# The forward convolution of a two-layer SSM kernel, reordered: tables between h chunks, table turns between spectra, the first norm of q inside the convolution, two residuals inside the inverse

## The chip, the cores and the metric

The kernel runs on one core of one Trainium2 chip. The metric is the device time of one launch in microseconds (us), the median of three runs: 986.35 us before the change (981.84, 986.35 and 989.6). One launch computes the forward pass of four layers and the gradients of all ten inputs. Engines are named as in the profile: PE (TensorE), DVE (VectorE), ACT (ScalarE), POOL (GpSimd), SP (SyncE, which here only issues DMAs).

## The reference, cut to what matters

```python
def A(q, k, v, shift_k, ssm_k, ssm_D):             # S = 2048 tokens, D = 512 channels
    k_shift = short causal conv of k with shift_k, four taps
    kv = k_shift * v
    y = irfft(rfft(kv padded to 2S) * rfft(ssm_k padded to 2S))[:S] + kv * ssm_D
    return q * y

def B(x, w1, b1, w2, b2):                          # F = 1376
    return gelu(x @ w1 + b1) @ w2 + b2

x = A_q
x = x + A(layernorm(x), A_k, A_v, ...)             # layer 0
x = x + B(layernorm(x), ...)                       # layer 1
x = x + A(layernorm(x), A_k, A_v, ...)             # layer 2, the same k, v and filter
x = x + B(layernorm(x), ...)                       # layer 3
# returned: x, and its vjp with grad_out for q, k, v, shift_k, ssm_k, ssm_D, w1, b1, w2, b2
```

The convolution's result y doesn't depend on x, so it is computed once for layers 0 and 2. Layer 0 then is: norm of q, times y, plus q.

## The kernel before, in words

The kernel has four phases: the forward convolution (`phase_conv_forward`), the forward pass of the layers and then the backward pass (both in `phase_mlp`), and the backward convolution with the weight gradients in its gaps. The change is to the first phase and to the start of the second.

**The transform.** The Fourier transform of length 4096 is done with matmuls. The tokens lie in four blocks of 512; the second half of each block is held in reversed order, which is why q, v and grad_out are first copied in DRAM with some rows reversed (`flip_rows`, one DMA of 1 MB each). The frequencies are cut into five groups by their rest k1 (`GROUPS`, 2, 2, 4, 4 and 4 tiles of 128 frequencies). For each group DVE combines blocks to "streams" (class `Fold`: tiles fold_x, fold_s, fold_d, fold_t), and PE multiplies them with a table of cosines and sines (`fwd_group`: PSUM tile sp_ps, evicted by ACT). There are two tables: tabN at integer positions, for the filter ssm_k (called h), and tabF at half positions, for kv. `sin_of` makes a quarter of a table: POOL and DVE compute phases into tab_u, DVE masks them, ACT takes the sine. For the way back the tables are needed transposed: `turn_table` makes tabI from tabF, `turn_integer_table` makes tabG from tabN, with transposes on PE and evictions on ACT or DVE.

**The order of phase one.** Tables tabN and wdiag (the short filter as diagonals); `h_chunk` for each of four channel chunks, which turns h (hA, hR), and the reversal of hR (hB); small tables sp5; the fold of h; `k_slice` for four blocks of k, which turns k; then

```python
    h_group(0)
    h_group(1)
    for i in range(4):
        ks_slice(i)
    h_group(2)
    ...                                      # tabF, turn_integer_table
    h_group(3)
    h_group(4)
```

`h_group` makes a group of spectra of h in pairs of tiles (Hg, two buffers) and stores each pair to DRAM (Hspec) from SP's queue. `ks_slice` does the short convolution with 64 small matmuls per block, multiplies with v on DVE to kv and stores ks from POOL's queue; v and ks have two buffers each (vt, ksb). kv is kept in the memory of y (tile y_res). Then tabI is turned, and the loop over the groups runs: load the h spectra (Hg of the inverse), `fwd_group` for kv (KVg), `inv_group` of the group before (iv_ps to W), `product` of the two spectra (pr_t, pr_u to Yg, one buffer), and the streams of a later group. At the end class `InvBlocks` sums up W on DVE and writes y, block by block.

**The start of phase two.** `phase_mlp` turns the weights on PE, then runs four lanes, one for each block of 512 tokens, interleaved by hand-set weights. A lane loads its part of q (x_sl), does the norm (`ln_slice`: bn_stats and bn_aggr on DVE, a power of -0.5 on POOL, scale and shift on DVE or ACT), stores the normalised n for the backward pass, multiplies with y and adds x (`a_fwd`), norms again, turns n by DMA, and does the dense layer with its gelu in groups of four 128-row chunks (`b_fwd`, `gelu_group`).

**What sets the order.** A scheduler places instructions, but PE and DVE work in phase one goes through the `Ordered` wrapper, which keeps the order of the program. Its helper is line 55, so all these instructions carry L55 in the profile and are told apart by their tiles. In phase one the name `tt` is taken from the plain engine, so the kv product (L491) is placed by the scheduler. Pools opened with `reuse_waits="tile"` wait only for the tiles whose memory they take over; others wait for the whole pool that had the memory.

Of the kernel before, what the change touches and what calls it, by code (L numbers as in the profile page):

```python
# [71 lines left out]
def ssm_kernel(ctx, tc: tile.TileContext, aps: dict):  # L72
# [10 lines left out]
    res.rstd = [const_pool.tile([P, NT], F32, name=f"rstd{i}") for i in range(4)]  # L83
    dram = Dram()
# [4 lines left out]
    dram.tabI = drampool.tile([P, 2, 16, 256], BF16, name="tabI_d")  # L89
# [11 lines left out]
    flip_rows(nc, dram.qB, qf, 511)  # L101
# [71 lines left out]
def sin_of(nc, consts, pool, out, krow, pv, shift, np_=P):  # L173
    n = krow.shape[-1]
    for c0 in range(0, n, 1024):
        w = min(1024, n - c0)
        u = pool.tile([P, 1024], I32, name="tab_u", tag="tab_u", bufs=2)[0:np_, 0:w]
        eng = nc.gpsimd if c0 == 0 else nc.vector
        eng.tensor_scalar(out=u, in0=krow[:, c0:c0 + w], scalar1=pv, scalar2=float(shift), op0=ALU.mult, op1=ALU.add)
        nc.vector.tensor_single_scalar(out=u, in_=u, scalar=8191, op=ALU.bitwise_and)  # L180
        nc.scalar.activation(out=out[:, c0:c0 + w], in_=u, func=ACT.Sin, scale=SIN_SCALE, bias=consts.pibias[0:np_, :])


def turn_table(nc, psum, consts, tab, dest, f, qt):

    for k0 in (0, 8):
        ps = psum.tile([P, 8, P], BF16, name="tt_ps", tag="kt", bufs=2)
        for k in range(8):
            nc.tensor.transpose(out=ps[:, k, :], in_=tab[:, f, qt, (k0 + k) * P:(k0 + k + 1) * P], identity=consts.ident)
        if f == 0:  # L190
            nc.scalar.activation(out=dest(k0), in_=ps, func=ACT.Identity)
        else:
            nc.vector.tensor_copy(out=dest(k0), in_=ps)


def turn_integer_table(nc, psum, pool, consts, tabN, dest):

    for f in range(2):
        for k0 in (0, 8):
            tg = pool.tile([P, 8, 2, P], BF16, name="tg", tag="kn", bufs=4)  # L200
            for qt in range(2):
                ps = psum.tile([P, 8, P], BF16, name="tn_ps", tag="kt", bufs=2)
                for k in range(8):
                    nc.tensor.transpose(out=ps[:, k, :], in_=tabN[:, f, qt, (k0 + k) * P:(k0 + k + 1) * P],
                                        identity=consts.ident)
                nc.scalar.activation(out=tg[:, :, qt, :], in_=ps, func=ACT.Identity)
            nc.gpsimd.dma_start(out=dest[:, f, k0:k0 + 8, :].rearrange("p k (t q) -> p k t q", t=2), in_=tg)
# [24 lines left out]
class Fold:  # L232


    def __init__(self, nc, pool, lo, hi, integer, X=None):
        tt = nc.vector.tensor_tensor
        self.nc, self.pool, self.integer = nc, pool, integer
        if X is None:
            X = pool.tile([P, 2, 4, 1024], BF16, name="fold_x", tag="fold_x", bufs=1)
# [61 lines left out]
def product(nc, pool, A, B, Rb, g, out, conj):  # L301
# [4 lines left out]
    for h in range(0, n, 2):  # L306
        s = slice(h, h + 2)
        t = pool.tile([P, 2, 2, 512], BF16, name="pr_t", tag="pr_t", bufs=2)
# [8 lines left out]
        tt(out=out[:, 0, s], in0=t[:, 0], in1=t[:, 1], op=op_r)  # L317
        tt(out=out[:, 1, s], in0=u[:, 0], in1=u[:, 1], op=op_z)
# [16 lines left out]
def inv_group(nc, psum, tabI, Y, g, W):  # L335
    k1, base, n = GROUPS[g]
    sr, sz = SLOT[k1]
    for m in range(2):
        q = slice(m * P, (m + 1) * P)
        for slot, (a, b) in ((sr, (0, 1)), (sz, (1, 0))):  # L340
# [3 lines left out]
            for kt in range(n):  # L344
                nc.tensor.matmul(ps[:, 0, :], lhsT=tabI[:, 0, base + kt, q], rhs=Y[:, a, kt, :], start=(kt == 0),
                                 stop=(kt == n - 1))
            for kt in range(n):
                nc.tensor.matmul(ps[:, 1, :], lhsT=tabI[:, 1, base + kt, q], rhs=Y[:, b, kt, :], start=(kt == 0),
# [46 lines left out]
def phase_conv_forward(ctx, nc, tc, dims, consts, dram, res, aps):  # L395
# [3 lines left out]
    h_ap = aps["A_ssm_k"]  # L399
    tt = nc.vector.tensor_tensor  # L400
    nc = Ordered(nc, tc, ("tensor", "vector"))
# [5 lines left out]
    wpool = res.wstack.enter_context(tc.tile_pool(name="wfwd", bufs=1, side="right"))  # L407
    rstack = ExitStack()
    tabs = rstack.enter_context(tc.tile_pool(name="cf_tab", bufs=1, side="right"))
    tabF = tabs.tile([P, 2, 2, 2048], BF16, name="tabF")  # L410
    foldp = rstack.enter_context(tc.tile_pool(name="cf_fold", bufs=1, side="right"))
    gen = ExitStack()
# [10 lines left out]
    hN = foldp.tile([P, ND * S + 16], BF16, name="hN", tag="fold_x", bufs=1)  # L423
    nc.vector.memset(hN[:, ND * S:ND * S + 16], 0.0)
    for cc in range(ND):
        nc.sync.dma_start(out=hN[:, cc * S:(cc + 1) * S], in_=h_ap[cc * P:(cc + 1) * P, :])
    for i in range(4):
# [5 lines left out]
    flip_rows(nc, dram.vB, v_ap, 511)  # L433

    krow = gp.tile([P, 2048], F32, name="krow")
    for k1, base, n in GROUPS:
        ki = gp.tile([P, 1024], I32, name="krow_i", tag="tab_u", bufs=2)[:, 0:n * P]
        nc.gpsimd.iota(ki, pattern=[[8, n * P]], base=k1, channel_multiplier=0)
        nc.vector.tensor_copy(out=krow[:, base * P:(base + n) * P], in_=ki)
# [10 lines left out]
    for qt in range(2):  # L450
        for f in range(2):
            sin_of(nc, consts, gp, tabN[:, f, qt, :], krow, pvn[:, qt:qt + 1], 2048 * (1 - f))
    wshf = gp.tile([P, ND, 4], F32, name="wshf")
    nc.vector.tensor_copy(out=wshf, in_=wsh)
    wdiag = gp.tile([P, ND, 4, P], BF16, name="wdiag")
    for cc in range(ND):
        for j in range(4):
            nc.vector.tensor_scalar(out=wdiag[:, cc, j, :], in0=consts.ident, scalar1=wshf[:, cc, j:j + 1],
# [878 lines left out]
```

## Time and profile before

| | of 985.4 us |
|---|---|
| PE busy | 803.6 (82%) |
| DVE busy | 729.5 (74%) |
| ACT busy | 611.6 (62%) |
| POOL busy | 152.5 (15%) |
| mean DMA rate | 180 GB/s |
| first spectrum of h on PE | starts at 51.6 |
| first spectrum of kv on PE | starts at 154.6 |
| last write of y on DVE | ends at 232.8 |
| first gelu operation on DVE | starts at 268.8 |
| last forward matmul of the chain | ends near 495 |

The table's lower half is read from the instructions in order of time. A share of busy time over the whole span says little here, since the phases have different limits: until 100 us the tables and the turns of k and h, then the transforms, then the layers. What an edit is worth has to be read from the stretch it lies in: which engine is full there, and which wait ends last. Idle time in front of an instruction stands in square brackets in the timeline, with what ended it.

### The profile page before, as it was taken

How to read it: one execution, taken by the hardware profiler on the slowest of the kernel's cores; microseconds unless marked ns; L12 is line 12 of the kernel's file. 1: busy time of each engine (PE TensorE's matmuls, PEld its weight loads, DVE VectorE, ACT ScalarE, POOL GpSimd, SP SyncE). 2: the span in 40 equal slices, each digit the busy share in tenths (PEclk: the TensorE clock that was granted, in tenths of full speed). 3: DMA queues.
4: the chain of work that ended last, by engine and by line, in shares of the span. 5: the costliest groups of instructions: out<-in, count | busy, mean ns of one | idle time of the engine just before them, and what ended most of it. 6: DMA issues, size and time to landing. Idle time of an engine off the chain costs nothing.

```text
span 985.4 us, 12825 instructions
## 1 busy us (share of the span) xinstructions
PE 803.6 (82%) x4677; PEld 411.7 (42%) x4754; DVE 729.5 (74%) x1207; ACT 611.6 (62%) x806; POOL 152.5 (15%) x271
## 2 busy tenths in 40 slices
PE   0686867984378777777899999978999998995998
PEld 0443424442133322333344444434455554853664
DVE  6624508787899999995847778895369997499873
ACT  5734724642599888987964654535566557753664
POOL 5421100000221112210001112222010304210000
PEclk9867988987698887898999999979999999997999
DMA  6067636303435555468699886647346688863331
GB/s 213 23 214 240 235 122 249 144 27 108 128 109 163 155 161 160 127 191 234 186 302 261 239 222 199 202 145 282 134 160 229 221 318 293 290 200 81 113 97 37
DMA packets 153415, 177.72 MB, mean 180 GB/s; under 512 B 50117, under 2 KB 133768, under 8 KB 152712
## 3 DMA queue, kind: packets, MB, share of 16 engines
q1 hardware_dynamic: 141816, 136.75, 45.0%
q0 software_dynamic: 11536, 40.15, 11.2%
q8 instruction: 37, 0.61, 0.3%
q14 instruction: 26, 0.21, 0.1%
HBM read 92.61 MB, written 82.13 MB: 177 GB/s over the span
## 4 chain that ended last, share of the span: by engine, by line
PE 38%; DVE 35%; ACT 9%; DMA 7%; issue 5%; POOL 4%; SPq 1%; ACTq 0%; DVEq 0%; POOLq 0%
PE sp_ps L55 8%; PE gh_ps L1013 6%; PE gn_ps L1031 6%; DVE Wb L55 6%; PE dw_ps L55 5%; DVE ln_st L897 3%; PE gh_ps L55 3%; DVE b1a L55 2%; DVE g_o L967 2%; PE iv_ps L55 2%; DMA Hspec_d<-Hg 2%; DMA kTc<-kT_d 2%; DMA tabFb<-tabF_d 2%; DVE pr_u L55 2%; PE dw_tp L55 1%
## 5 line engine op out<-in xcount | busy, mean ns | idle before, releaser
L55 PE MATMUL dw_ps<-G,dw_tm 128*128 128x512 bf16 x672 | 167.9, 385 | 4.8 <-ACT dw_tm L1133 3.0
L1133 ACT ACTIVATE dw_tm<-dw_tp 128x1024 bf16<-128x1024 bf16 x88 | 89.9, 1024 | 70.7 <-PE dw_tp L55 70.7
L996 PE MATMUL o_ps<-w_sb,h_sl 128*128 128x512 bf16 x343 | 95.3, 421 | 39.7 <-DVE h_sl L966 38.8
L984 PE MATMUL z_ps<-nT_sl,w_sb 128*128 128x512 bf16 x346 | 83.4, 395 | 20.7 <-DMA nT_sl<-n_sl 19.1
L55 PEld LDWEIGHTS <-dw_tm 128*128 128x128 bf16 x704 | 65.3, 99 | 64.1 <-ACT dw_tm L1133 3.7
L1015 ACT ACTIVATE gz_sl<-gh_ps 128x512 bf16<-128x512 f32 x88 | 50.2, 594 | 55.4 <-PE gh_ps L1013 52.2
L1031 PE MATMUL gn_ps<-w1T_sb,gz_sl 128*128 128x512 bf16 x345 | 80.7, 379 | 0.6 <-DVE gz_sl L1016 0.3
L1013 PE MATMUL gh_ps<-gT_sl,w2T_sb 128*128 128x512 bf16 x344 | 79.1, 379 | 0.5
L996 PEld LDWEIGHTS <-h_sl 128*128 128x128 bf16 x352 | 36.5, 107 | 93.7 <-DVE h_sl L966 44.7
L984 PEld LDWEIGHTS <-w_sb 128*128 128x128 bf16 x352 | 35.0, 101 | 73.5 <-DMA nT_sl<-n_sl 28.3
L986 ACT ACTIVATE g_z<-z_ps,b1col 128x512 bf16<-128x512 f32 x88 | 54.2, 688 | 12.7 <-PE z_ps L984 12.7
L55 PEld LDWEIGHTS <-dw_fm 128*128 128x128 bf16 x704 | 48.3, 100 | 21.5 <-issue 1.9
L55 PE MATMUL dw_tp<-ident,dw_fm 128*128 128x128 bf16 x704 | 55.3, 223 | 0.0
L962 ACT ACTIVATE g_s<-g_t 128x2048 bf16<-128x2048 bf16 (+1 forms) x24 | 42.5, 1771 | 18.2 <-DVE g_t L961 18.2
L1031 PEld LDWEIGHTS <-gz_sl 128*128 128x128 bf16 x352 | 34.3, 98 | 42.0 <-DVE gz_sl L1016 1.0
L1013 PEld LDWEIGHTS <-w2T_sb 128*128 128x128 bf16 x352 | 34.3, 98 | 41.2
L55 DVE TENSOR_REDUCE b1a<-dw_fm 128x1 f32<-128x2048 bf16 x22 | 49.6, 2279 | 0.0
L900 POOL TENSOR_SCALAR rstd<-ln_mv 128x4 f32<-128x4 f32 x16 | 11.4, 715 | 233.1 <-DVE ln_mv L898 148.8
L1043 POOL TENSOR_SCALAR bb_diag<-ident,bb_cols 128x128 bf16<-128x128 bf16 x32 | 21.6, 674 | 152.7 <-DVE bb_junk L1040 143.6
L897 DVE BATCH_NORM_STATS2 ln_st<-x_sl 128x6 f32<-128x512 bf16 x64 | 42.0, 670 | 2.9 <-DMA x_sl<-in_A_q_dram 2.8
L1016 DVE TENSOR_TENSOR gz_sl<-gz_sl,gpb 128x2048 bf16<-128x2048 bf16 (+1 forms) x24 | 27.2, 1135 | 21.5 <-DMA gpb<-gp_d 11.4
L959 ACT ACTIVATE g_q<-g_z 128x2048 bf16<-128x2048 bf16 (+1 forms) x24 | 42.8, 1783 | 0.1
(289 smaller groups left out, 1633.2 us busy)
## 6 DMA issues: line engine op xcount, KB each, us to landing
dw_fm<-h_d SPq DMA_DIRECT2D x22, 512.0 KB, 5.1
dw_fm<-gz_d SPq DMA_DIRECT2D x22, 512.0 KB, 3.8
n_d<-n_sl SPq DMA_DIRECT2D x16, 512.0 KB, 3.6
h_d<-h_sl SPq DMA_DIRECT2D x16, 512.0 KB, 2.9
gp_d<-g_p SPq DMA_DIRECT2D x16, 512.0 KB, 3.2
nb_sl<-n_d SPq DMA_DIRECT2D x16, 512.0 KB, 4.6
gpb<-gp_d SPq DMA_DIRECT2D x16, 512.0 KB, 5.8
gz_d<-gz_sl SPq DMA_DIRECT2D x16, 512.0 KB, 4.9
```

The source lines that it names most:

```text
L55: return self.tc.keep_in_program_order(f(*args, **kwargs))
L897: nc.vector.bn_stats(out=st, in_=x[:, t, :])
L959: nc.scalar.activation(out=q, in_=zb, func=ACT.Square)
L962: nc.scalar.activation(out=sg, in_=t, func=ACT.Sigmoid)
L984: nc.tensor.matmul(ps, lhsT=w.w1[:, dc, c * P:(c + 1) * P], rhs=nT[:, dc, :], start=(dc == 0), stop=(dc == ND - 1))
L986: nc.scalar.activation(out=zb[:, c - c0, :], in_=ps, func=ACT.Identity, bias=w.b1col[:, c:c + 1])
L996: nc.tensor.matmul(ps, lhsT=h[:, c, t * P:(t + 1) * P], rhs=w.w2[:, c, :], start=False, stop=(c == NFC - 1))
L1013: nc.tensor.matmul(ps, lhsT=w.w2T[:, dc, c * P:(c + 1) * P], rhs=gT[:, dc, :], start=(dc == 0), stop=(dc == ND - 1))
L1015: nc.scalar.activation(out=gz[:, c, :], in_=ps, func=ACT.Identity)
L1016: nc.vector.tensor_tensor(out=gz[:, c0:c0 + k, :], in0=gz[:, c0:c0 + k, :], in1=gp[:, 0:k, :], op=ALU.mult)
L1031: nc.tensor.matmul(ps, lhsT=gz[:, c, t * P:(t + 1) * P], rhs=w.w1T[:, c, :], start=(c == 0), stop=(c == NFC - 1))
L1133: nc.scalar.activation(out=dst, in_=ps, func=ACT.Identity)
```

## The change

It moves work within the forward convolution, and pulls the start of layer 0 into it. Part by part:

- One quarter of tabN is made ahead of each `h_chunk`, wdiag behind them. tab_u gets three buffers, and DVE's masks are done in reversed order.
- The streams of h are made ahead of the groups that use them. h groups 0 and 1 stand behind ks slices 0 and 1; a quarter of tabF is made behind each ks slice.
- All table turns become a list of units (`table_turns`), four behind each pair of h tiles in groups 2 and 3. tabI is four tiles in the memory of vt and ksb.
- Stores of h spectra are issued from ACT instead of SP. The products of kv go through the ordered engine.
- q is loaded into the memory of kv once it is folded, normed there (`norm_load`, `norm_sums`, `norm_apply`) and stored as n; lanes 2 and 3 behind the first kv spectrum, lanes 0 and 1 inside the loop.
- Yg is split into halves with three buffers; pr_t has one buffer instead of two. The weights are loaded from inside the loop's program (`start_weights`), and the two small DVE operations on them come later (`finish`).
- `first_sum` does the product with y, the residual and the statistics of the second norm for lanes 0 and 1 between the sums of the inverse. x of all lanes is one tile, loaded in the loop into the memory of fold_x.
- Three pools of phase two wait by tile instead of by pool, and the backward pass has a pool of its own for g_sl.

It is meant to keep PE and DVE supplied in the front part and to take the first norm out of the start of the layers. The diff, cut to its core:

```diff
@@ sin_of
-        u = pool.tile([P, 1024], I32, name="tab_u", tag="tab_u", bufs=2)[0:np_, 0:w]
+        u = pool.tile([P, 1024], I32, name="tab_u", tag="tab_u", bufs=3)[0:np_, 0:w]
...
@@ phase_conv_forward
-    tt = nc.vector.tensor_tensor
     nc = Ordered(nc, tc, ("tensor", "vector"))
+    tt = nc.vector.tensor_tensor
...
-    for qt in range(2):
-        for f in range(2):
-            sin_of(nc, consts, gp, tabN[:, f, qt, :], krow, pvn[:, qt:qt + 1], 2048 * (1 - f))
...
     for cc in range(ND):
+        qt, f = cc // 2, cc % 2
+        sin_of(nc, consts, gp, tabN[:, f, qt, :], krow, pvn[:, qt:qt + 1], 2048 * (1 - f))
         h_chunk(cc)
...
+    sth = [fh.streams(GROUPS[0][0]), fh.streams(GROUPS[1][0])]
...
+    turns = table_turns(nc, psum, gp, consts, tabN, dram.tabG, tabF, tabI, dram.tabI)
+
+    def h_group(g, nturns=0):
         k1, base, n = GROUPS[g]
-        st = fh.streams(k1)
         for h0 in range(0, n, 2):
             H = hrot.tile([P, 2, 2, 512], BF16, name="Hg", tag="Hg", bufs=2)
-            fwd_group(nc, psum, tabN, st, g, H, extra, h0, h0 + 2)
-            nc.sync.dma_start(out=dram.Hspec[:, :, base + h0:base + h0 + 2, :], in_=H)
+            fwd_group(nc, psum, tabN, sth[g], g, H, extra, h0, h0 + 2)
+            nc.scalar.dma_start(out=dram.Hspec[:, :, base + h0:base + h0 + 2, :], in_=H)
+            for _ in range(nturns):
+                turns.pop(0)()
...
-    h_group(0)
-    h_group(1)
     for i in range(4):
         ks_slice(i)
-    h_group(2)
...
+        if i < 2:
+            h_group(i)
+        if i in (1, 3):
+            sth.append(fh.streams(GROUPS[(i + 3) // 2][0]))
+        tabF_part(i)
...
+    h_group(2, 4)
+    h_group(3, 4)
+    sth.append(fh.streams(GROUPS[4][0]))
...
     h_group(4)
-    res.w = start_weights(nc, wpool, dims, aps)
...
+    norm_load(2)
+    norm_load(3)
     load_spec(0)
     load_spec(1)
...
-    sts = [fk.streams(GROUPS[0][0]), fk.streams(GROUPS[1][0])]
+    sts = [fk.streams(GROUPS[0][0])]
+    spectrum(0)
+    norm_sums(2)
+    norm_sums(3)
+    norm_apply(2)
+    norm_load(0)
+    norm_apply(3)
+    norm_load(1)
+    sts.append(fk.streams(GROUPS[1][0]))
...
-        Ys.append(invp.tile([P, 2, 4, 512], BF16, name="Yg", tag="Yg", bufs=1))
-        product(nc, invp, KV, H, Rb, g, Ys[g], False)
+        Ys.append([invp.tile([P, 2, 2, 512], BF16, name="Yg", tag="Yg", bufs=3) for _ in range(n // 2)])
+        product(nc, invp, KVs[g], H, Rb, g, Ys[g], False)
...
+        if g == 0:
+            norm_sums(0)
+            norm_sums(1)
+            res.w = start_weights(nc, wpool, dims, aps)
+        if g == 1:
+            norm_apply(0)
+            norm_apply(1)
+        if g == 2:
+            res.w.finish()
+    res.x = res.xpool.tile([P, NT, D], BF16, name="x_sl", tag="fold_x", bufs=1)
+    for s in range(4):
+        tok_io(nc, res.x[:, s * TS:(s + 1) * TS, :], aps["A_q"].flatten_outer_dims(), dram.qB, s)
...
+    def first_sum(s):
+        x, n = res.x[:, s * TS:(s + 1) * TS, :], ns[s % 2]
+        tt(out=n, in0=n, in1=res.y[:, s * TS:(s + 1) * TS, :], op=ALU.mult)
+        tt(out=x, in0=n, in1=x, op=ALU.add)
+        res.ln1[s] = norm_stats(nc, invp, res.mhalf, x, res.rstd[1], s, res.nmr1[:, s * TS:(s + 1) * TS])
+
+    res.ln1 = {}
+    first_sum(0)
     for m in range(2):
         ib[m].others()
-        for i in range(1, 4):
+    for i in range(1, 4):
+        for m in range(2):
             ib[m].out(i, yv[:, :, m], yv[:, :, 2 + m])
+        if i == 1:
+            first_sum(1)
@@ phase_mlp
-        m.small = st.enter_context(tc.tile_pool(name="m_small", bufs=2))
-        m.spool = st.enter_context(tc.tile_pool(name="m_s", bufs=1))
-        m.hpool = st.enter_context(tc.tile_pool(name="m_h", bufs=1))
+        m.small = st.enter_context(tc.tile_pool(name="m_small", bufs=2, reuse_waits="tile"))
+        m.spool = st.enter_context(tc.tile_pool(name="m_s", bufs=1, reuse_waits="tile"))
+        m.hpool = st.enter_context(tc.tile_pool(name="m_h", bufs=1, reuse_waits="tile"))
...
-                x = m.spool.tile([P, TS, D], BF16, name="x_sl", tag=f"x{s}", bufs=1)
-                tok_io(nc, x, q_ap, dram.qB, s)
+                x = res.x[:, s * TS:(s + 1) * TS, :]
```

## The prediction, written before the result was known

> **What bounds the kernel now.** I first cut the span into stages by what they compute and asked for the busy time of every engine in each (columns: stretch, length, then busy us and instruction count of PE, PEld, DVE, ACT and POOL, granted clock, DMA share, GB/s).
>
> ```profile
> 0.00:51.60 51.60, 18.24 (x141) 13.06 (x142) 33.26 (x83) 32.45 (x52) 26.71 (x69) 0.89 0.33 113
> 51.60:103.90 52.30, 43.73 (x320) 23.29 (x322) 15.93 (x19) 23.51 (x30) 8.19 (x17) 0.72 0.65 228
> 103.90:154.60 50.70, 35.70 (x208) 17.87 (x210) 19.15 (x28) 22.17 (x23) 3.23 (x6) 0.83 0.47 176
> 154.60:213.00 58.40, 50.66 (x213) 21.70 (x218) 46.65 (x68) 30.69 (x36) 0.00 (x0) 0.94 0.43 162
> 213.00:232.90 19.90, 14.65 (x110) 8.68 (x111) 19.42 (x36) 11.17 (x18) 0.00 (x0) 0.83 0.00 1
> 232.90:268.80 35.90, 14.11 (x64) 5.91 (x63) 26.44 (x61) 13.05 (x19) 8.53 (x20) 0.71 0.51 150
> 268.80:330.00 61.20, 44.52 (x172) 18.37 (x177) 58.71 (x89) 58.28 (x60) 12.55 (x16) 0.86 0.45 140
> ```
>
> The rows are: tables and the turning of h; spectra of h and the short conv; the rest of the h spectra with the table turns; spectra of kv, products and inverse (called the loop below); the inverse's last sums; first norms and residuals up to the first gelu operation; gelu of the first lanes. PE has most to do in rows two to four, DVE is full in row five, DVE and ACT both are in row seven. Nothing is full in row six, a start-up of 35.9 us.
>
> Then I read the chain of waits in order of time: in rows two and three it passes through stores.
>
> ```profile
> 50.31 1.24 DVE fold_t L55
> 70.24 7.51 DMA ks_d<-ksb
> 119.12 13.23 DMA Hspec_d<-Hg
> 142.43 3.04 DMA Hspec_d<-Hg
> 223.61 2.02 DVE y_res L55 x6
> 234.74 4.05 DMA x_sl<-qB_d
> 239.09 1.06 POOL rstd L901
> ```
>
> One 512 KB store of h spectra takes 13.2 us, while the list of issues has 3.8 us as its median. The next h spectra wait for its buffer, and the inverse pool waits for the last store. The same stretch among the waits shows who paid, and the timeline shows that the loop's end is tied by one product buffer:
>
> ```profile
> DVE tabI L55 <- DMA Hg<-Hspec_d: 25.1, 1, 25.1
> ACT Hg L298 <- DMA Hspec_d<-Hg: 8.2, 1, 8.2
> 200.78 0.69 DVE L55 TENSOR_TENSOR Yg<-pr_t 128x1024 bf16<-128x1024 bf16 x1 [6.63 <-PE iv_ps L55]
> 205.07 3.15 PE L55 MATMUL iv_ps<-Yg,tabI 128*128 128x512 bf16 x7 [2.93 <-DVE Yg L55]
> ```
>
> DVE stood still for 25.1 us before the table copies. The product of the last group waited 6.6 us for PE to let go of the one Yg; then PE waited 2.9 us for that product.
>
> [...] the 13.2 us store was issued on SP at 119.1, behind the reversed copy of grad_out issued on SP at 111.9, while the transfer rate lay near 100 GB/s. [...] a 128x512 matmul takes 0.38 us from 98 us on and 0.6 us after the 5.2 us pause at 133; but from 51.6 to 98 us the PE stays slow although it is nearly always busy, so I don't count on a better clock. [...] tensor_tensor in bf16 takes 1224 ns at 2048 elements. The trace has 1.22 us.
>
> **The change part by part.**
>
> 1. Tables between h chunks. In row one DVE makes all integer tables (10.6 to 22.0), then wdiag (to 24.9), then the evictions of hA from 25.1, so that PE stands idle for 18 us. Interleaved, a round costs 2.1 us of tables and 1.7 of evictions on DVE, 2.3 and 1.2 on ACT: four rounds end near 25, wdiag near 28, hB's eight evictions (4.3 us of ACT) near 30. The third tab_u buffer shortens the ten small sp5 rounds (37 to 42 now). fold_x starts near 35 instead of 43.5, and its 9 us lie beside the k slices (13 us of ACT, 30 to 43) and the first ks slice, which now precedes the first h group. PE starts this work near 43 instead of 51.6: 8.5 us.
>
> 2. Rows two and three. The matmuls and turns are the same, 79.4 us of PE busy time in 103 us; 23.6 are idle. By the waits: 3.8 for a ks buffer, 4.1 for fold_d, 3.0 for the turns behind ACT, 4.7 for turns behind tabI (held by the last Hspec store), 1.9 for fold_t, 5.2 for an Hg buffer. The new order (ks slices between h groups, turns behind each h pair, stores from ACT, tabI in the vt and ksb slots) puts other matmuls into each of these. New waits: v's third load stands on SP behind the lane of the first two Hspec stores, which lands it near 78; behind it on DVE stand the third kv product and the table work that ACT needs between two Hg evictions, so ACT and then PE lose 3 to 5 us. Each of eight stores costs ACT an issue, of the order of the 0.5 us that SP shows; ACT has 46 us of work here in 103. I take 4 us. The loop starts 8.5 + 23.6 - 4 = 28 us earlier, near 126.6.
>
> 3. The norm of q. Per lane: four stats at 0.66 us (in step with their aggregates), four applies at 0.35: 4.1 us. Lanes 2 and 3 (8.2 us) run while PE does the last two h groups and DVE has nothing: free. Lanes 0 and 1 lie in the loop, with 1.4 us of weight memsets and b2 work: 9.6 us more on a DVE that has 46.7 of 58.4. The second product is queued behind the 6.2 us of stats and memsets, and PE's inverse of group 1 and the spectrum of group 3 wait for it: PE falls some 5 to 8 us behind, and gets back 3.7 of its last waits from Yg in three halves. DVE's sum, 56 us, still fits. I book 3 us of loss (0 to 7). x for the residual is loaded into fold_x after the last streams, hidden by 20 us of loop.
>
> 4. Two residuals in the inverse. Row five is all DVE. It gains 2 x (2.46 for two tensor_tensor + 2.65 of stats) = 10.3 us: 30.2 instead of 19.9.
>
> 5. Row six. No load (2.8 us), no POOL waits for the norm of q (2.3, 2.1 and 2.1), no norm of q, and lanes 0 and 1 done. DVE goes into the residual of lane 2 at once. ACT's order puts the first normalisation of lane 2 in front of the first g_z, so that the first gelu operation waits for: residual of lane 2 and statistics with part of lane 3's, 6.6 us; POOL, 2; three n_sl, five g_z and one g_q on ACT, 8. That is 16.6 instead of 35.9: 19.3 gained.
>
> 6. Row seven. Before, DVE still does all of lane 3's first norm and residual here (6.6) and the second statistics of lanes 2 and 3 (about 4.4): 11 us less in a stretch where DVE had 58.7 of 61.2. But ACT has 58.3: I count the 11 because ACT too comes ahead (n_sl of lanes 0 to 2 are behind it).
>
> Sum: 28 - 3 - 10.3 + 19.3 + 11 = 45 us. Backward and weight gradients don't change in work: their 493 us move up whole. 986.35 - 45 = 941.
>
> **The rivals.** (a) PE stays slow for the whole front and the turns don't fit: row three's warm 10.3 us per four h tiles becomes the 14.4 of group 2 for two groups and the 16 turns take 0.95 instead of 0.65 us, 8 + 5 = 13 us lost: 954. For it: clock 0.72 in row two. Against: row three ran warm until its stop. (b) ACT bounds row seven and part 6 gives nothing, with some loss in the loop (7 rather than 3) and half of (a): 941 + 11 + 4 + 7 = 963. For it: 58.3 of 61.2. (c) PE warms up because it no longer pauses: the four ks slices (5.5 us each) and the first two h groups (12.3 together) at 0.38/0.6 of their time and group 2 at row three's 10.3 save 8 + 4.5 + 4 = 16.5: 925. For it: the slow stretch is preceded by pauses. (d) Slower. [...] at 7.5 us (as for ks_d above) for eight stores that is 60 us, with the 9.6 us of the loop exposed: 941 + 60 + 7 = 1008. [...]
>
> **How the numbers follow.** Forecast 0.50, (a) 0.19, (b) 0.12, (c) 0.14, (d) 0.05. The likeliest gives 941. The range 923 to 965 takes in (a), (b) and (c) and leaves (d) out; with the spread of the forecast itself some 0.16 lies outside. One per cent is 976.5: all but (d) and the edge of (b) lie below. Faster 0.92, same 0.04, slower 0.04.
>
> **What would show it.** Part 1: first h spectrum's fold_x near 35, first ks matmul near 43. Part 2: first KVg near 128, no Hspec store over 6 us, PE idle under 10 us before it. Part 3: q's stats of lanes 2 and 3 in front of the first product with no PE wait behind; a PE wait for Yg of group 1 in the loop. Parts 4 and 5: inverse sums of about 30 us and first g_t 16 to 17 us behind them. Part 6: ACT, not DVE, without gaps after the first g_s. It is wrong if ACT shows waits between Hg evictions for DMA, or if the start of the backward (now at 492) doesn't move up by 35 us or more.

## The result, and the profile after

The changed kernel takes 956.33 us (median of 4 runs, 954.27 to 959.16), the kernel before 984.66 us in the same comparison: a ratio of 0.971 with a 95% interval of 0.966 to 0.976. It is 28 us faster; forecast were 45, with 941 us and a range of 923 to 965. The profiled spans are 985.4 and 952.4 us, 33 us apart; the sums below use these. (The profiled execution after is the shortest of its four runs and the one before lies above the median of its own, hence 33 and not 28.)

The stages of the changed kernel, in the columns of the table shown for the kernel before. Rows one to six are the same work, with the stretches moved to where each stage now begins: start, h spectra and short conv, rest of h and table turns, loop, the inverse's last sums, start of the layers up to the first gelu operation. The last three rows are the forward layers from there on.

```profile
0.00:45.40 45.40, 21.37 (x142) 14.85 (x143) 34.58 (x83) 31.39 (x51) 26.44 (x65) 1.00 0.61 205
45.40:80.00 34.60, 29.61 (x324) 20.56 (x323) 19.71 (x25) 23.51 (x31) 11.67 (x21) 0.98 0.68 237
80.00:117.60 37.60, 33.59 (x208) 14.70 (x207) 22.31 (x39) 24.39 (x26) 8.73 (x17) 0.97 0.85 312
117.60:180.30 62.70, 51.75 (x249) 22.90 (x249) 56.52 (x97) 33.93 (x40) 4.22 (x8) 1.00 0.64 219
180.30:211.50 31.20, 16.97 (x112) 9.30 (x111) 30.38 (x56) 12.69 (x22) 6.33 (x8) 0.79 0.19 51
211.50:227.80 16.30, 11.49 (x38) 4.29 (x38) 10.28 (x22) 10.66 (x16) 4.34 (x8) 0.78 0.38 89
227.80:290.00 62.20, 48.73 (x197) 20.08 (x197) 54.10 (x65) 58.94 (x61) 2.38 (x4) 0.92 0.47 146
290.00:380.00 90.00, 68.10 (x277) 27.89 (x275) 81.23 (x120) 78.41 (x82) 8.63 (x18) 0.87 0.44 138
380.00:462.80 82.80, 59.93 (x242) 24.84 (x243) 58.18 (x73) 63.62 (x70) 5.56 (x11) 0.86 0.61 176
```

Read the PE and clock columns of rows two and three first: 63.2 us of PE work in 72.2, where before it was 79.4 in 103, and a granted clock of 0.98 and 0.97 instead of 0.72 and 0.83. Then the last two rows: in the last one neither PE, DVE nor ACT is full, and in the one before it DVE comes nearest, with 81.2 of 90 us.

The chain of waits in order of time (start, length, what) no longer passes through a store in the convolution; it ends in the layers at a DMA turn:

```profile
45.40 4.83 PE ks_ps L55 x64
...
107.46 10.20 PE sp_ps L55 x40
117.69 1.03 ACT Hg L314
...
217.94 1.17 POOL rstd L989
...
303.48 1.87 SPq L1043
305.40 2.70 DMA nT_sl<-n_sl
308.35 3.59 PE z_ps L1087 x8
```

Stage by stage, in us (the stretch is counted here from the start of the first gelu operation to the end of the last forward matmul):

| | before | after | change | forecast |
|---|---|---|---|---|
| start to the first kv spectrum | 154.6 | 117.6 | -37.0 | -28 |
| loop | 58.4 | 62.7 | +4.3 | +3 |
| last sums of the inverse | 19.9 | 31.2 | +11.3 | +10.3 |
| start of the layers | 35.9 | 16.3 | -19.6 | -19.3 |
| first gelu to last forward matmul | 226.5 | 235.0 | +8.5 | -11 |
| rest (backward) | 490.1 | 489.6 | -0.5 | 0 |
| sum | 985.4 | 952.4 | -33.0 | -45 |

So the first gelu operation comes 41 us earlier, more than the 34 forecast, and 8.5 us are given back in the 235 us behind it. The waits of that stretch (engine and line, what it waited for, us in total, times, longest) say where. First of the kernel before:

```profile
PE z_ps L984 <- DMA nT_sl<-n_sl: 12.1, 6, 4.5
ACT g_z L986 <- PE z_ps L984: 5.3, 6, 3.3
```

Then of the changed one:
```profile
ACT g_z L1089 <- PE z_ps L1087: 27.6, 11, 7.9
PE z_ps L1087 <- DMA nT_sl<-n_sl: 27.2, 5, 8.3
```

PE waits 27 us for turned activations, ACT then waits 28 us for PE. These are waits on the way of one lane from its first dense layer to the second (residual, two norms, DMA turn), when nothing of the other lanes stands ready ahead of it. The experiments ask why; they will show too that the sum of such waits doesn't tell how long the stretch is.

### The profile page after: what moved, and what is told of

Same layout as the page of the kernel before. It is cut to its first block, busy times and chain, and to the rows that moved or that the text cites. A ratio compares the mean times of both kernels' runs of the same rounds, so it can differ in the third digit from the quotient of the medians.

```text
span 952.4 us, 12919 instructions
## 1 busy us (share of the span) xinstructions
PE 794.6 (83%) x4754; PEld 406.6 (43%) x4754; DVE 734.0 (77%) x1203; ACT 613.5 (64%) x810; POOL 151.7 (16%) x274
## 4 chain that ended last, share of the span: by engine, by line
PE 37%; DVE 30%; ACT 17%; DMA 6%; issue 6%; POOL 3%; SPq 1%; ACTq 0%; DVEq 0%; POOLq 0%
PE gn_ps L1134 7%; PE sp_ps L55 7%; PE gh_ps L1116 6%; DVE Wb L55 6%; PE dw_ps L55 6%; ACT g_z L1089 3%; PE gh_ps L55 3%; DVE b1a L55 3%; ACT g_s L1065 3%; ACT g_o L1066 2%; ACT g_q L1062 2%; DVE pr_t L55 2%; DVE pr_u L55 2%; PE z_ps L1087 2%; DMA tabFb<-tabF_d 2%
## 5 line engine op out<-in xcount | busy, mean ns | idle before, releaser
L55 PE MATMUL dw_ps<-G,dw_tm 128*128 128x512 bf16 x704 | 170.8, 381 | 2.2 <-ACT dw_tm L1236 2.2
L1087 PE MATMUL z_ps<-nT_sl,w_sb 128*128 128x512 bf16 x352 | 93.8, 424 | 32.3 <-DMA nT_sl<-n_sl 27.2
L1099 PE MATMUL o_ps<-w_sb,h_sl 128*128 128x512 bf16 x352 | 92.1, 404 | 26.7 <-DVE h_sl L1069 26.4
L1087 PEld LDWEIGHTS <-w_sb 128*128 128x128 bf16 x352 | 37.3, 107 | 88.4 <-issue 43.0
L1089 ACT ACTIVATE g_z<-z_ps,b1col 128x512 bf16<-128x512 f32 x88 | 55.2, 708 | 27.6 <-PE z_ps L1087 27.6
L989 POOL TENSOR_SCALAR rstd<-ln_mv 128x4 f32<-128x4 f32 x16 | 7.6, 475 | 248.1 <-DVE ln_mv L987 161.9
L1146 POOL TENSOR_SCALAR bb_diag<-ident,bb_cols 128x128 bf16<-128x128 bf16 x32 | 21.6, 676 | 157.3 <-DVE bb_junk L1143 148.1
L1066 ACT ACTIVATE g_o<-g_t 128x2048 bf16<-128x2048 bf16 (+1 forms) x24 | 42.7, 1780 | 0.0
```

The lines of the kernel that those rows point to most:

```text
L55: return self.tc.keep_in_program_order(f(*args, **kwargs))
L1066: nc.scalar.activation(out=o, in_=t, func=ACT.Sigmoid, scale=-1.0)
L1087: nc.tensor.matmul(ps, lhsT=w.w1[:, dc, c * P:(c + 1) * P], rhs=nT[:, dc, :], start=(dc == 0), stop=(dc == ND - 1))
L1089: nc.scalar.activation(out=zb[:, c - c0, :], in_=ps, func=ACT.Identity, bias=w.b1col[:, c:c + 1])
L1099: nc.tensor.matmul(ps, lhsT=h[:, c, t * P:(t + 1) * P], rhs=w.w2[:, c, :], start=False, stop=(c == NFC - 1))
```

## The experiments

Unless a diff says otherwise each is an edit of the changed kernel. The table holds the landmarks from each profile, in us: start of the first kv spectrum, of the first gelu operation and of the last forward matmul group, and the stretch between the last two. Kernels with a ratio have four runs, and the ratio is to the kernel before in the same comparison (medians of 984.7 to 990.5 us); the others have a single run, and what is read from them is read from their profile.

| kernel | time | ratio to before | first kv | first gelu | last matmul | stretch |
|---|---|---|---|---|---|---|
| before | 984.66 | 1 | 154.6 | 268.8 | 494.9 | 226.1 |
| changed | 956.33 | 0.971 (0.966 to 0.976) | 117.6 | 227.8 | 462.4 | 234.6 |
| e1_lane_order | 965.41 | 0.978 (0.975 to 0.981) | 118.4 | 230.3 | 470.7 | 240.4 |
| e2_before_lane_order | 997.34 | 1.010 (1.006 to 1.014) | 151.9 | 267.6 | 505.6 | 238.0 |
| e3_h_first | 958.51 | | 120.0 | 232.2 | 466.6 | 234.4 |
| e4_sp_stores | 969.82 | | 128.0 | 243.0 | 477.0 | 234.0 |
| e5_no_first_sum | 961.46 | | 117.6 | 227.2 | 466.7 | 239.5 |
| e6_norm1_dve | 965.02 | 0.978 (0.971 to 0.985) | 119.0 | 237.2 | 470.6 | 233.4 |
| e7_norm13_dve | 954.79 | 0.967 (0.961 to 0.973) | 118.0 | 234.4 | 461.3 | 226.9 |
| e8_yg_two | 960.85 | | 118.8 | 234.3 | 469.0 | 234.7 |
| e9_tables_first | 957.05 | | 117.0 | 229.9 | 463.5 | 233.6 |
| e10_hand_order | 946.50 | 0.961 (0.958 to 0.965) | 118.0 | 228.3 | 453.2 | 224.9 |
| e11_hand_norm_dve | 951.10 | 0.966 (0.963 to 0.970) | 116.1 | 229.5 | 454.9 | 225.4 |
| e12_hand_free_start | 953.78 | 0.967 (0.961 to 0.972) | 116.1 | 234.4 | 457.9 | 223.5 |

### The lanes: is it their order?

**e1_lane_order.** Lanes 0 and 1 now skip the first layer's steps, and with them 7 units of the weights that interleave the lanes; lanes 2 and 3 skip 4. The edit undoes that.

```diff
-            lanes = [(s * 12.0, fwd(s)) for s in range(NSL)]
+            lanes = [(s * 12.0 + (7.0 if s in m.ln1 else 4.0), fwd(s)) for s in range(NSL)]
```

> The changed kernel with lane offsets of 7, 19, 28 and 40 instead of 0, 12, 24 and 36, which gives the lanes' steps the same order as in the kernel before (less the norms of q that are gone). Theory L (the four lanes lost their old order, because lanes 0 and 1 skip 7 units of weight at the start and lanes 2 and 3 only 4; some lanes now run so close together that PE waits for the DMA turns of nT): the stretch from the first gelu operation to the last forward matmul falls from 235 us to 226.5 (its length before) or a little less, PE's waits for nT from 27 us to under 20, and the time from 956 to about 948. Theory R (the stretch is longer for another reason, such as the single tile of x for all lanes or the pools that wait by tile): the stretch stays at 233 to 237 and the time at 954 to 959.

Measured: a stretch of 240.4 us and 965 us. It went the other way, so theory L falls in this form. PE's waits for nT did go down, to 5.9 us, and the stretch grew all the same. ACT now stands for 13.7 us in front of normalisations whose norm isn't there (316 to 423 us), and PE for 17.5 us in front of residuals that ACT has yet to finish (x_sl). The list of PE's instructions shows that the same program order of steps didn't bring back the order on the engine that the kernel before had; how the scheduler came to another one isn't shown.

**e2_before_lane_order.** The reverse edit in the kernel before.

```diff
-            lanes = [(s * 12.0, fwd(s)) for s in range(NSL)]
+            lanes = [(s * 12.0 - (7.0 if s < 2 else 4.0), fwd(s)) for s in range(NSL)]
```

> The kernel before with lane offsets of -7, 5, 20 and 32, which gives its lanes the order that they have in the changed kernel. Theory L: the stretch from the first gelu operation to the last forward matmul grows from 226.5 to about 235 us, with waits of ACT for z_ps of more than 15 us instead of 5, and the time from 985 to about 993. Theory R: no change, 226 us and 983 to 987. Its first part is that of the kernel before, so it also shows whether PE's slow matmuls between 51 and 98 us come again.

Measured: stretch 238.0 instead of 226.1, time up by 1.0%. Nothing but the order was changed. From the middle of the stretch on, PE's sequence of z and output matmuls in e2 is that of the changed kernel, and the list of waits of e2 has the two waits that the kernel before had only in small:

```profile
PE z_ps L984 <- DMA nT_sl<-n_sl: 24.6, 6, 9.2
ACT g_z L986 <- PE z_ps L984: 22.9, 16, 7.8
```

The order of the lanes can cost 12 us by itself. A single tile of x or the pools that wait by tile aren't needed to explain the loss, for this kernel has neither.

**e10_hand_order.** If order is the cause, an order written out by hand can cure it.

```diff
-            lanes = [(s * 12.0, fwd(s)) for s in range(NSL)]
-            interleave(lanes)
+            gens = [fwd(s) for s in range(NSL)]
+            for s in [0, 0, 0, 1, 2, 2, 1, 0, 1, 0, 0, 0, 0, 3, 3, 2, 1, 2, 0, 0, 1, 1, 1, 1, 0, 3, 2, 3, 1, 1,
+                      2, 2, 2, 2, 1, 0, 3, 0, 2, 2, 3, 3, 3, 3, 2, 1, 0, 1, 3, 3, 0, 0, 0, 0, 3, 2, 1, 2, 1, 1,
+                      1, 1, 3, 2, 3, 2, 2, 2, 2, 3, 3, 3, 3, 3, 0, 1, 2, 3]:
+                next(gens[s], None)
```

> The changed kernel with the steps of the four lanes listed by hand instead of by offsets and weights: next block's first gelu group, this block's last, next block's second, then this block's output matmuls, and each lane's second residual one block later. In the order of PE's instructions, 72, 83, 72 and 87 matmuls of other lanes' z then stand between a lane's last output matmul of the first dense layer and its first z of the second; before the change it was 88 in all four, in the changed kernel 44, 88, 56 and 44. Theory O (the order of the lanes sets the length of the gelu stretch, since the way of a lane between the layers has to be hidden by others): the stretch from the first gelu operation to the last forward matmul falls from 235 to 222 to 228 us and the time to 943 to 950. Rival (something else lengthens it): 233 or more, and 953 or more.

Measured: stretch 224.9 us, 946.5 us, ratio 0.961 (0.958 to 0.965). Theory O holds. The last matmul comes 9.2 us earlier with the first gelu 0.5 us later, and in the list of its waits that of PE's matmuls for turned activations is nearly gone:

```profile
PE z_ps L1087 <- DMA nT_sl<-n_sl: 3.8, 1, 3.8
```

Of the 9.7 us by which the stretch is shorter, 5.6 are idle time of PE (58.2 us in the changed kernel, 52.6 here); the other 4.1 are PE's busy time, 176.4 and 172.3 us for the same work. This is the fastest version. Note too the five kernels that keep the changed kernel's lanes (changed, e3, e4, e8, e9): their first gelu lies anywhere from 227.8 to 243.0 us, and the stretch behind it is 233.6 to 234.7 in all. It doesn't depend on when it starts.

### The lanes: is it ACT's work?

**e7_norm13_dve** and **e6_norm1_dve** move scale and shift of norms from ACT to DVE, e7 all 32, e6 twelve (there the condition is `l == 2 or (l == 1 and s < 3)`).

```diff
-        if l == 2:
+        if l in (1, 2, 3):
             nc.vector.tensor_scalar(out=n[:, t, :], ...
```

> The changed kernel with all scales and shifts of the norms in the layers on DVE: ACT loses 32 instructions of 0.81 us (26 us), DVE gains 32 of 0.41 us (13 us) on top of some 200 in a stretch of 235. Theory A (ACT's work bounds the stretch): the last forward matmul comes at 440 or before and the time is 930 to 940. Theory B (each lane's way between layers bounds it): the second half of the stretch still has waits of ACT for z_ps of 15 us or more, and the time is 945 or more[...].

> The changed kernel with the scale and shift of the first layer's second norm for lanes 0, 1 and 2 on DVE instead of ACT (twelve instructions of 0.41 us instead of 0.81). Theory A (ACT[...] is held for 10.4 and 5.6 us by normalisations of lanes 1 and 2 that wait for their norm, while z of lane 0 is ready; and ACT's work bounds the stretch): the first gelu operation comes at 211 to 217 instead of 227.8, and the time falls by 10 to 16 to 940 to 946. Theory B (the stretch is bound by the way of each lane from one dense layer to the next, not by ACT's start): the first gelu operation comes earlier, but the last forward matmul stays within 4 us of 462.4, and the time is 952 to 958.

Measured for e7: the stretch is 226.9 us, but the first gelu comes 6.6 us later, so the last matmul moves by 1.1 us only, and the time can't be told from the changed kernel's. ACT's wait for z_ps stays at 26.7 us, 17.5 of them in one piece. By its numbers theory B holds: taking 26 us of work off ACT bought no time. That ACT's work doesn't bound the stretch doesn't follow, though. The five kernels above show that a later start leaves the stretch at 234 us; e7's is 7.7 us shorter from its late start on, with as much of z still to do. So the edit did shorten the stretch, and DVE, which has the normalisations now, took the gain back in front of it: lane 0's starts there at 215.0, behind the inverse's sums, where ACT started it at 196.1. Whether ACT's load counted or the place of the normalisations in its queue isn't separated. Here is the whole stretch of e7 in the columns of the stage table (ACT is the fourth engine):

```profile
234.40:461.70 227.30, 170.84 (x705) 71.62 (x704) 198.76 (x273) 184.48 (x186) 16.13 (x32) 0.88 0.52 157
```

And the whole stretch of e10:
```profile
228.30:453.20 224.90, 172.28 (x717) 72.36 (x716) 192.19 (x256) 200.82 (x210) 24.46 (x32) 0.89 0.54 160
```

e10 does more ACT work in less time. For e6 both theories were off: the first gelu came at 237.2, 9.4 us later than before the edit, since DVE reaches lane 0's normalisation only after the inverse's sums, and lane 2's sits behind that. The time rose to 965.

**e11_hand_norm_dve** puts e7's edit on e10.

> The kernel of e10_hand_order with all scales and shifts of the norms in the layers on DVE, as in e7_norm13_dve: 26 us of work off ACT, 13 us more on DVE. Theory O: with the way between layers hidden, ACT's work counts again, so that the stretch becomes 8 us shorter or more than in e10_hand_order and the time lies below 942. Rival (ACT's work doesn't count, as in e7_norm13_dve): within 3 us of e10_hand_order.

Measured: stretch 225.4, 951.1 us, not faster than e10. The rival holds: with the hand order ACT's work isn't the limit; its gaps in front of g_s, up to 5.7 us, now wait for DVE. PE's waits for turned activations are longer here than in the changed kernel, and yet the stretch is 9 us shorter:

```profile
PE z_ps L1087 <- DMA nT_sl<-n_sl: 37.7, 3, 15.3
```

With e1's 5.9 us in the longest stretch of all, this rules out that the sum of PE's waits for the turns sets the length.

**e12_hand_free_start.** In the changed kernel the start looks like this on ACT (start, length, instruction; in brackets the idle time before it and what ended it):

```profile
211.34 0.81 ACT L1009 ACTIVATE n_sl<-x_sl,nmr,rstd 128x512 bf16<-128x512 bf16 x1 [10.37 <-POOL nmr L994]
...
220.87 0.81 ACT L1009 ACTIVATE n_sl<-x_sl,ln_nmr,rstd 128x512 bf16<-128x512 bf16 x1 [5.64 <-POOL ln_nmr L994]
221.59 0.67 ACT L1089 ACTIVATE g_z<-z_ps,b1col 128x512 bf16<-128x512 f32 x1
```

PE had started on z of lane 0 at 214.3, but ACT stood at normalisations of lanes 1 and 2. The edit, on e10, takes them and lane 3's off ACT:

```diff
-        if l == 2:
+        if l == 2 or (l == 1 and s > 0):
```

> The kernel of e10_hand_order with the scale and shift of the first layer's second norm on DVE for lanes 1, 2 and 3; lane 0 stays on ACT. In ACT's order the first g_z then follows the weights' evictions directly and isn't held by the norms of lanes 1 and 2 (10.4 and 5.6 us in e10_hand_order). Theory S (ACT's start is worth what it stands idle): first g_z at 204 to 208 instead of 222, and the time 4 to 12 us below e10_hand_order, 935 to 943. Rival D (DVE takes over as the gate: it has the inverse's sums, two residuals and now the three normalisations in front of the first gelu operation): first g_z early all the same, first gelu operation on DVE still at 225 to 231, and the time within 3 us of e10_hand_order, 944 to 950.

Measured: 953.8 us, and the first g_z came at 227.3, later than in e10. Neither theory foresaw that. The first line is from the timeline of SP, which issues the DMA turns:

```profile
195.74 20.51 SPq L1043 DMA_TRANSPOSE nT_sl<-n_sl  x2
```

The second is from the timeline of PE in the same kernel:
```profile
225.41 3.15 PE L1087 MATMUL z_ps<-nT_sl,w_sb 128*128 128x512 bf16 x7 [24.10 <-DMA nT_sl<-n_sl]
```

Two DMA turns take 20.5 us of SP's queue, until lane 1's normalisation on DVE, which starts at 214.6, has run. That a turn of lane 1 stands there ahead of the rest of lane 0's is read from this time; the trace doesn't name the lane. Freed from ACT's queue, the same wait came back in SP's.

### The residuals in the inverse

**e5_no_first_sum** takes out both `first_sum` calls; its lanes then have the order of e1.

```diff
-    first_sum(0)
...
-        if i == 1:
-            first_sum(1)
```

> The changed kernel without the residual sums of lanes 0 and 1 inside the inverse; all four lanes do them at their start, as before, with the norms of q still done in the convolution. All lanes then skip the same weight, so their order is that of e1_lane_order, with which it is compared. Theory B (as booked in the prediction: 10.3 us more in the inverse, given back in the start-up): the inverse's sums take 20 instead of 31 us, but the first gelu operation comes at 228 or later and the last forward matmul not before 470. Theory A (nothing is given back, since ACT stands waiting for norms at the start anyway): the first gelu operation comes at 217 to 224 and the last forward matmul at 460 to 466.

Measured: the sums are done at 200.1 instead of 211.5, and the first gelu comes at 227.2 instead of 227.8. Against the changed kernel, moving two residuals into the inverse costs 11 us there and gives back 11 in the start-up. That lies between the theories: nothing is lost by taking the residuals out, and the 4 us or more that A expected of it aren't gained, because ACT stands 16.9 us in front of the first normalisation instead. Against e1, which has the same order of the lanes and was meant for the comparison, the first gelu comes 3.1 us earlier and the last matmul 4.0, of which 0.8 stem from the convolution: a small loss by the residuals in the inverse isn't excluded by this single run. Its stretch, 239.5, is that of e1.

### The convolution

**e3_h_first** puts both h groups ahead of the first ks slice.

```diff
+    h_group(0)
+    h_group(1)
     for i in range(4):
         ks_slice(i)
-        if i < 2:
-            h_group(i)
```

> The changed kernel with h groups 0 and 1 ahead of the first ks slice, as in the kernel before; everything else as changed. Theory W (the ks slice ahead of the h groups is what brings PE to full speed by 49 us): the 128x512 matmuls of h groups 0 and 1 take about 0.6 us again, the ks slices about 0.3 us per 128x128 matmul, and the first spectrum of kv starts 8 us later or more, at 126 or after. Theory I (PE is fast because the pauses are gone, whatever comes first): the matmuls take 0.38 us within 5 us of the first h group, and the first spectrum of kv starts at 116 to 121.

Measured: first kv at 120.0. PE starts the h groups at 45.7 slow (0.6 us a matmul) and takes 0.38 us from 52.5 on. Theory I holds, but for 7 slow us instead of 5: the order of ks and h is worth 2.4 us, not 8.

**e4_sp_stores** issues the h spectra's stores from SP again (`nc.sync.dma_start` for `nc.scalar.dma_start`).

> The changed kernel with the stores of h spectra issued from SP again. Theory C (the slow store before was due to the reversed copy of grad_out in SP's row at that time, and that copy now comes later): every store lands within 6 us and the first spectrum of kv starts at 117.6 plus or minus 2. Theory Q (the queue decides whatever else is in it): one or more stores take over 8 us, and the first spectrum of kv starts at 122 or later.

Measured: first kv at 128.0, 10.4 us later. By the numbers theory Q came true. Theory C's number fails because its premise does: the reversed copy of grad_out doesn't come later, SP issues it at 77.5, one line ahead of the next store. The traces speak for the cause that C names, the copy ahead of a store on SP, and against "whatever else is in it": the two stores behind the copy took 25.6 and 11.0 us to land, the last two, at 124.0 and 129.1 and from SP as well, 3.0 and 3.6. A kernel with the stores on SP and the copy elsewhere wasn't run. First, from the list of DMA issues, the stores of the changed kernel from ACT (KB each, median us to landing):

```profile
Hspec_d<-Hg ACTq DMA_DIRECT2D x8, 512.0 KB, 5.9
```

The same list of e4, cut to 74 to 110 us (its median is that of the two landings just named):
```profile
Hspec_d<-Hg SPq DMA_DIRECT2D x3, 512.0 KB, 18.3
```

In the changed kernel the copy is issued from SP at 75.0 as well, and the eight stores from ACT land in 3.0 to 7.3 us. That a store issued from ACT wouldn't be held up behind the copy was, before these runs, the author's estimate: in the trace before all eight are on SP. The rate while the slow one of 13.2 us was on its way, said to be near 100 GB/s, was 158 on average (119.1 to 132.4 us), near 100 only until 125 and again from 129 (96 to 120). What a late store does to PE is seen in the timeline of PE in e4:

```profile
98.03 0.61 PE L55 MATMUL tt_ps<-ident,tabF 128*128 128x128 bf16 x8 [0.31 <-ACT tabI L200]
105.10 1.86 PE L55 MATMUL sp_ps<-fold_t,tabN 128*128 128x512 bf16 x4 [6.46 <-ACT Hg L314]
...
112.14 1.83 PE L55 MATMUL sp_ps<-fold_t,tabN 128*128 128x512 bf16 x4
...
117.68 1.03 PE L55 MATMUL sp_ps<-fold_t,tabN 128*128 128x512 bf16 x4
```

After 6.5 us of waiting, four matmuls take 1.86 us instead of 1.03, and go on slowly until 113.9.

**e9_tables_first** makes all four quarters of tabN ahead of the h chunks, wdiag still behind them.

```diff
         sin_of(nc, consts, gp, tabN[:, f, qt, :], krow, pvn[:, qt:qt + 1], 2048 * (1 - f))
+    for cc in range(ND):
         h_chunk(cc)
```

> The changed kernel with all four quarters of the integer tables ahead of the four h chunks, as before; the rest as changed. Theory T (part 1 of the prediction: the tables between the chunks bring PE's start forward by several us): the first ks matmul comes at 50 to 53 instead of 45.2, and the first spectrum of kv at 122 to 126 instead of 117.6. Rival (the turning of k and ACT's queue set the start anyway): 45 to 47, and 117 to 120.

Measured: first ks matmul at 46.2, first kv at 117.0. The rival holds: the tables between the chunks are worth 1 us at most at the first ks matmul, and nothing at the first kv. What brought the start forward is seen in the timeline of DVE, first of the kernel before:

```profile
22.15 2.76 DVE L55 TENSOR_SCALAR wdiag<-ident,wshf 128x128 bf16<-128x128 bf16 x16
24.88 0.31 DVE L55 MEMSET kT<- 128x128 uint32 x2
25.11 1.21 DVE L55 CAST hA<-ha_ps 128x512 bf16<-128x512 f32 x2
...
43.45 4.49 DVE L55 TENSOR_TENSOR fold_x<-hA,hB 128x4096 bf16<-128x4096 bf16 x2
```

Then of e9:
```profile
21.50 1.28 DVE L55 CAST hA<-ha_ps 128x512 bf16<-128x512 f32 x2
...
29.29 2.69 DVE L55 TENSOR_SCALAR wdiag<-ident,wshf 128x128 bf16<-128x128 bf16 x16
...
38.57 4.49 DVE L55 TENSOR_TENSOR fold_x<-hA,hB 128x4096 bf16<-128x4096 bf16 x2
```

With wdiag and the memsets out of the way the evictions of h start 3.6 us earlier: 3.1 for the time that those took, and 0.4 because the tables, still made in one go, end at 21.6 instead of 22.0. Between there and fold_x another 1.3 us are saved, where the sp5 rounds stand; that this is the third tab_u buffer wasn't tried alone.

**e8_yg_two** gives Yg two half buffers.

```diff
-name="Yg", tag="Yg", bufs=3)
+name="Yg", tag="Yg", bufs=2)
```

> The changed kernel with two half buffers of Yg instead of three, which is the one whole buffer of the kernel before. As booked (three halves give back 3.7 us in the loop): the loop from the first spectrum of kv to the first of the inverse's last sums takes 66 us or more instead of 62.7, with DVE waiting over 5 us for iv_ps at the last product. Rival (the last product waits for PE anyway): 62 to 64 us.

Measured: the loop takes 67.9 us (118.8 to 186.7), 5.2 more, and the wait at the last product is the old one. From the timeline of DVE in e8:

```profile
174.52 0.69 DVE L55 TENSOR_TENSOR Yg<-pr_t 128x1024 bf16<-128x1024 bf16 x1 [6.44 <-PE iv_ps L55]
```

In the changed kernel:
```profile
171.60 0.69 DVE L55 TENSOR_TENSOR Yg<-pr_t 128x1024 bf16<-128x1024 bf16 x1 [2.90 <-PE iv_ps L55]
```

## Why the prediction was right, and where it was wrong

The direction and the range held, and the sizes of steps 3, 4 and 5 were right to about a microsecond. The sum holds two errors of opposite sign, 9 us too little in the convolution and 19.5 us too much in the layers. That they cancel in part is luck: with the error of the layers alone the result would have been near 960, 5 us from the range's upper end.

1. **Tables between h chunks.** The start moved from 51.6 to 45.2 (43 forecast), fold_x from 43.5 to 37.6 (35 forecast). Some three quarters of the size came, but for another reason: by e9 the tables' place gives 1 us, and by the timelines moving wdiag and the memsets behind the chunks gives about 3.
2. **Rows two and three.** PE's idle time fell from 23.6 to 9.0 us; 4 were forecast, and the sign given (under 10) held. The failed term is "The matmuls and turns are the same, 79.4 us of PE busy time": they took 63.2. That is rival (c), which had put 16.5 us on it; 16.2 were measured. The forecast had set a better clock aside on a wrong reading, that PE stays slow from 51.6 to 98 us although it is nearly always busy. It isn't so: in the trace before, PE gets fast within the ks slices and is granted the full clock from 68 us on; behind the pause of 3.9 us in front of 78.5 it is slow again (a granted clock of 0.50 until 80, 0.69 from 80 to 82), and the slow stretch from 89.5 to 98 (0.50) stands behind the pause of 4.2 us for fold_d. Three windows of the kernel before, cut to the ks matmuls (the columns here are stretch, length, PE busy us and count, granted clock, DMA share, GB/s), show the change:

```profile
66.00:67.00 1.00, 1.00 (x12) 0.50 0.92 336
67.00:68.00 1.00, 1.00 (x16) 0.72 0.97 251
68.00:69.00 1.00, 1.00 (x22) 1.00 1.06 372
```

That the pauses make PE slow is argued from these runs: e2, with the pauses of the kernel before and the same convolution, needs 76.9 us for the same PE work, so that 2.6 of the 16.2 us may be a difference of executions; e4, which has one pause of 6.5 us, needs 67.9; the changed kernel, whose longest pause is 2.8 us with slow matmuls until 2.6 us behind it, 63.2. No new waits on ACT for DMA showed between the Hg evictions (the 4 us priced for ACT's delays were an estimate), and rival (d) is out: its 7.5 us of ACT for each store were an estimate from the landings of ks_d, and the eight issues on ACT took 0.52 to 0.57 us each. Stores took up to 7.3 us to land, where none over 6 was foretold. Of the 30.8 us that rows two and three gained, stores from ACT are worth 10.4 (e4) and the order of ks and h 2.4 (e3); the turns behind the h pairs, the tables behind the ks slices and tabI's new place weren't taken out alone.
3. **Norm of q.** The loop grew by 4.3 us (3 forecast, 0 to 7). PE waits 3.5 us for Yg of group 1, as said; the third half of Yg gives back 5.2 (e8; 3.7 booked).
4. **and 5. Residuals.** 31.2 us of sums (30.2) and 16.3 of start-up (16.6). The two terms are about a zero sum as far as the first residuals go: e5 has neither and reaches the first gelu at the same time. What is left of row six's gain is the norm of q and its load: in e5 that row takes 27.1 us with all four residuals in it, 8.8 less than before.
6. **The gelu stretch: this step failed.** It took 11 us less of DVE work for 11 us less of time, "because ACT too comes ahead". The stretch grew by 8.5 instead. DVE's work in it did fall, from 201.5 to 193.1 us, and ACT's from 202.2 to 200.6, so less work didn't make it shorter. What the runs show in its place is the order in which the lanes' instructions stand in the engines' queues: e2 shows that this order alone costs 12 us in the kernel before, and e10 that another order gives 9.7 us back with ACT's work unchanged. That a good order hides each lane's way between the layers behind matmuls of other lanes fits these waits, but it is argued: e11 has longer waits for the turns than the changed kernel in a short stretch. Nor is the order the only lever: e7 shortens the stretch by 7.7 us with the steps of the lanes as they were. So rival (b), which had the result (963 against 956) by ACT's load, isn't out for the changed order, where that load and the order may act together; with the hand order it is (e11: 225.4 against 224.9 us). The foretold sign, ACT without gaps after the first g_s, didn't come: ACT waits 27.6 us for z_ps there. The prediction worked out every edit of the diff and left out that skipping steps shifts the weights that interleave the lanes.

The sign at the end was met by its letter: the start of the backward moved up by 32 us, less than the 35 named, and the cause was part 6.

What stays open is why e1, with the old order of steps, got another order of instructions than the kernel before, and a worse one. Only the outcome is shown.

## What to carry to other kernels

Work taken off an engine may shorten a stretch and still buy no time, since it stands in front of something else on the engine that takes it over (e7). ACT was busy for 58.3 of the first 61.2 us, but for 202 of the 226 us of the whole stretch, so look at the whole of it and ask which wait would remain. The sum of one engine's waits isn't a measure of the loss either: PE's waits for the turns were 5.9 us in the longest stretch and 37.7 in a short one. Where lanes are interleaved by weights, an edit that removes steps from some of them changes the order for all; compare the order on each engine, and try one written out by hand if it has gone bad. An instruction that waits for a later lane can hold what is ready behind it, on ACT (10.4 and 5.6 us in the changed kernel) as in SP's queue (20.5 us in e12), and moving it to another queue moved the wait along.

## What the runs showed of the hardware

The same instructions of the kernel before ran at different speeds in two executions. The timeline of PE has, in the kernel before:

```profile
63.77 10.90 PE L55 MATMUL ks_ps<-wdiag,kT 128*128 128x128 bf16 x160
```

And in e2, whose convolution is the same:
```profile
62.08 9.11 PE L55 MATMUL ks_ps<-wdiag,kT 128*128 128x128 bf16 x160
```

In e2 PE got fast 7 us after its start at 52.0, before these matmuls; in the kernel before it stayed slow (a granted clock of 0.50 from 51.6 to 67) for 16 us of nearly unbroken work, until 67.7, in the midst of them. The runs here show slow matmuls (about 0.6 us at 128x512 instead of 0.38) until 2.6 us after a pause of 2.8, for 7 us in e2 and e3, for 9 us after the pause of 6.5, and once for 16. Rows two and three gained more than the idle time that was closed: 14.6 us of it went, and with it 16.2 us of busy time, of which some 2.6 may be the difference between two executions that e2 shows.
